# A tuned list scheduler replaced by an explicit order of all operations, and the first MLP group passed on by two token tiles

## The chip, the cores and the metric

The kernel runs on one core of one Trainium2 chip. The metric is device time in microseconds (us) of one execution, lower is better. Each kernel is run several times, and always beside runs of the kernel before on the same chip. Such runs have a state, fast or slow. A ratio is the mean time of one kernel's fast runs over that of the kernel before in the same rounds, so it isn't quite the ratio of the medians quoted beside it.

## The reference, cut to what matters

One block of a network on 2048 tokens of 640 columns: a layer norm with modulation, a long convolution by Fourier transform (length 4096) gated by `q`, a residual, then a gated MLP whose gate is mixed over tokens.

```python
h = _layernorm(x) * (1 + ca) + sa
x = x + ga * _A_ref(h, A_k, A_v, A_shift_k, A_ssm_k, A_ssm_D)   # taps, k*v, FFT convolution, times h
h = _layernorm(x) * (1 + cb) + sb
# _B_ref:
z  = _gelu(h @ w_in)
z1 = z[..., :Fh]                                 # Fh = 864
z2 = _layernorm(z[..., Fh:])                     # over Fh
g  = einsum('ts,bsf->btf', w_sp, z2) + b_sp      # "the mix": every output tile needs all 16 token tiles of z2
x  = x + gb * ((z1 * g) @ w_out)
```

## The kernel before

The first half of the kernel (convolution, second norm, MLP up to the gelu) is not written as instructions in order. It is written as about 950 operations, each with what it reads and writes, the engines that may do it, and a planned cost in ns for each engine. A list scheduler with hand-searched priorities (`WANT`, `SHIFT`, `SECOND`) then emits them one by one:

```python
while len(order) < len(ops):
    found = []
    for i in ready:
        ...                                   # earliest start on each engine that may do it
        if e == "POOL" or (e == "DVE" and o["port"]):
            at = max(at, port)                # the plan's own model of the shared port
    best = min((f for f in found if f[1] <= first + LOOK), default=None)
    ...
    if e == "PE":
        self.gap = max(0, int((at - max(last, freed[i]) - 300) * 0.7 / 217))   # dummy matmuls to keep the clock
    o["fn"](engines[e])                       # emits the instruction
```

A token group is four tiles of 128 tokens. From the second group on, the normed tokens are turned by a transposing transfer from one buffer `Z` into another:

```python
def turn(e):
    new(hT, "Z", [P, TB, ND, P])
    e.dma_start_transpose(tl[hT][...], tl[xn2][...])       # Z <- Z
op({"SP": 2900}, turn, r=[xn2], w=[hT], new=[(hT, "Z")], flip=True)
```

and each gate tile is normed on VectorE when its group's `rstdz` is there:

```python
op({"POOL": 1300}, lambda e: rstd_from_var(rstdz[...], mvz[...]), w=[("rsz", g)])   # a power, on GpSimd
for i, n in enumerate(ns):
    op({"DVE": 500}, lambda e: e.tensor_scalar(z2[i], z2[i], mvz[n], rstdz[n], op0=subtract, op1=mult), port=True)
```

What follows the plan is ordinary code, which the change leaves alone, and which the plan doesn't know:

```python
w_o = wsp_pool.tile([P, NFT, D], BF16, name="w_o")
for ft in range(NFT):                                      # 7
    nc.sync.dma_start(w_o[...], B_w_out[...])
    nc.gpsimd.tensor_tensor(w_o[...], w_o[...], gb_bf[...], op=ALU.mult)
for t in range(NT + 2):
    if t < NT: mix(t)                                      # sums over all 16 tiles of z2, tile 0 first
    ...
```

Of the kernel before, what the change touches and what calls it, by code (L numbers as in the profile page):

```python
# [9 lines left out]
ACT = mybir.ActivationFunctionType  # L10
# [29 lines left out]
LAND = 1700  # L40
LOOK = 42
# [4 lines left out]
WANT = {  # L46
    "f1": 2526.25, "m2": -2037.5, "e": -1944.5, "g2": -1880.25, "sc": -2044.75, "kv0": -1374, "kv1": 127.25,
    "kv2": 1518, "kv3": 2314.5, "kv4": -3404.75, "taps0": -2491.5, "taps1": -157, "taps2": -1900, "taps3": 1990.75,
    "taps4": 2196.25, "kvw0": -1376.75, "kvw1": 1291.5, "kvw2": -1942.25, "kvw3": 2716, "kvw4": 2479.5, "XK0": -1183,
    "XK1": -1620.25, "XK2": 2217, "XK3": 2063, "XK4": 2051.5, "XU0": -1237, "XU1": -1437.75, "XU2": 1801,  # L50
    "XU3": -1000, "XU4": -1551, "k0": -2274, "k1": 89, "k2": -860.25, "k3": -849, "k4": -2326.5, "fk0": -246,
    "fk1": -1040.5, "fk2": -2275, "fk3": -687, "fk4": -1166.75, "u0": -1617.75, "u1": -1000.75, "u2": -1876,
    "u3": -3389.75, "u4": -849.5, "x0": -165.25, "x1": -853, "x2": 1266.5, "x3": 1164, "ln": 928.25, "xn": -1205,
    "gh0": 788.5, "gh1": -1692, "gh2": 2045.75, "gh3": 1665.5, "gh4": 4149.25, "mod2": 1139.5, "mod1": 1538,
    "mod0": 2027, "silu": 3015.75, "mod3": 4190.5, "mod4": 1313, "mod5": -1137.75, "w_in1": 3051, "w_in0": -489.75,
    "zt0": 2475, "zt1": -229, "zt2": -1076.5, "zt3": -1427.5, "zt4": -1724, "y0": -2303.5, "y1": -1549, "y2": -210.5,
    "y3": -1942.5, "y4": 2310.75, "res0": -1928.75, "res1": 1888.5, "res2": 2026, "res3_0": -1974.25,
    "res3_1": -1926.75, "res3_2": 1516.5, "res3_3": -1289.25, "res4_0": 1282.75, "res4_1": 1349.25, "res4_2": 2307.5,
    "res4_3": -2318.5, "st1": 4181.5, "st3_0": 1263.25, "st3_1": 2953.5, "st3_2": 2321, "st3_3": 3037,
    "st4_0": -1125.75, "st4_1": 1295, "st4_2": -1307.25, "st4_3": -2593, "zp_0": -1343, "zp_1": -802.25,  # L60
    "zp_2": -1300.5, "zp_3": -2354.5, "zx_0": 1146, "zx_1": -299.75, "zx_2": -1879, "zx_3": -1309.25, "zf_0": -1226.5,
    "zf_1": -1880.25, "zf_2": 1818, "zf_3": -1874, "z2_0": -1075.75, "z2_1": -1726, "z2_2": -1235, "z2_3": 2149,
    "zs_0": 1156.75, "zs_1": 2527.75, "zs_2": -147.25, "zs_3": -1292.5, "zn_0": 1300.75, "zn_1": 1666.75,
    "zn_2": 1139.25, "zn_3": 1283.5, "z1_0": -1946.5, "z1_1": -1925.5, "z1_2": 1809, "z1_3": 2464.75,
}


SHIFT = {
    0: 29.25, 1: 33.25, 2: 6.25, 4: -16, 5: 31, 6: -36, 7: 19, 9: 40.25, 12: -40.75, 13: -24, 14: 34, 15: -121.5,
    16: 52.25, 17: -75.75, 18: 0.25, 20: -0.75, 21: 2.75, 22: 39.25, 23: -15.25, 24: 41.5, 25: -1, 27: 6, 28: -4.75,  # L70
    29: 96.5, 30: 8.75, 31: 10.5, 32: 17, 33: -0.5, 35: 0.75, 36: -6.75, 37: 27, 38: -5.5, 39: -1.5, 40: -30.5,
    41: -38.5, 42: -2.75, 43: -47.75, 44: -21.5, 46: 29.75, 47: 37.25, 48: -6, 49: 7.75, 50: 15.5, 51: -14.75,
    52: 11.5, 53: -104.25, 55: 4.75, 56: -9.75, 57: 6.75, 58: 11, 59: -79.25, 60: 15.5, 61: -9, 62: 52.5, 63: 131.75,
    64: 2.5, 65: 7.25, 67: -21, 68: 5, 70: -50.75, 71: 5.25, 72: -74.75, 73: -87.25, 74: 10.25, 75: -19.25, 76: -2.75,
    77: -5, 78: -11.75, 79: -0.75, 80: 1.75, 82: 9, 83: -47.75, 84: 5.75, 85: 90.75, 86: -60, 89: 159.5, 91: 0.5,
    92: -68.25, 93: -11.75, 95: -1.75, 96: 11, 97: 99.75, 98: 113, 99: -1, 100: -26.5, 101: -461.5, 102: 64.75,
    103: -36.75, 104: -24.75, 105: 53, 106: 51, 107: 183.75, 108: 70.25, 109: 10.25, 110: -104.75, 111: -11.5,
    112: 35, 114: 5.25, 116: 0.5, 117: -5.75, 120: 5.5, 121: 7.25, 122: 51.75, 123: 11, 124: -2.75, 125: -104,
    126: 63.25, 127: 44.75, 128: 110.5, 129: -35.25, 130: 97.25, 131: 64.25, 132: -82.5, 135: 3.75, 136: 0.5,
    137: 30.75, 138: -2.5, 139: 12.75, 140: 1.75, 141: 15.5, 143: -1.25, 144: -23.5, 146: 207, 147: 185.5,  # L80
    148: -16.75, 149: 29.5, 151: 39.75, 152: 23, 153: 9.5, 154: -6.5, 155: 1.75, 156: -61.5, 157: 38.75, 158: -49.25,
    159: 0.5, 160: -72.25, 161: -111.75, 162: -10, 164: -19, 165: -71, 166: -2.5, 170: 128, 171: -49.75, 172: -64.5,
    173: -77.75, 174: -4.25, 175: 0.5, 176: 51, 177: -13.5, 178: -8, 179: -27, 180: -33, 181: -207.25, 182: 5.25,
    183: -11, 185: -20.5, 186: 35.5, 187: -38.25, 189: -0.5, 192: -12.75, 193: -0.25, 194: -1.75, 196: -0.25,
    197: -13.75, 199: -12.75, 200: -21, 201: -55.25, 202: 26.75, 203: -26.75, 204: -2.75, 205: 1, 206: 21.25, 207: -1,
    208: 44.5, 209: -11.75, 210: 0.75, 211: -3.25, 214: 22.75, 216: 13, 217: -6.25, 218: -16.5, 219: 1.5, 220: 59.75,
    221: -3.25, 222: 2.5, 223: -26.25, 224: 64.5, 225: -39.25, 227: -3.75, 228: -4.25, 229: -59.75, 230: 22.25,
    231: 52.25, 232: 157.25, 235: -10, 236: 17, 237: -1.25, 238: 11.75, 239: 87.25, 240: 14.5, 241: -0.75, 242: -4.25,
    243: -8.5, 244: -9.5, 245: 3.5, 246: 1, 247: 425, 249: 35.25, 250: -5, 251: -0.5, 252: 41.5, 253: 81, 254: 1,
    256: -94.5, 257: 157.5, 259: 575.5, 260: -41.75, 263: 8.5, 265: 6.5, 266: 55, 267: -2.5, 268: 84.5, 270: -18,  # L90
    272: -5.25, 273: 101, 276: 113.5, 277: -26, 278: 15.75, 279: -26.5, 281: 10.75, 283: 32.75, 285: 6.75, 286: 63.75,
    287: 23.25, 288: 2.25, 289: -24.5, 291: -6.5, 292: 10.25, 293: 0.5, 294: -53.25, 295: 19.5, 296: 1.5, 297: 0.75,
    298: -14.75, 299: -1.5, 300: 57.25, 302: -1, 304: -42, 305: 7.25, 306: -51.25, 307: 17.75, 309: -36.75, 310: -2.5,
    311: 3, 312: 45.25, 313: 4, 314: 17.5, 315: 3.25, 317: -3.5, 318: 22, 319: 43, 320: -28.5, 321: -0.5, 322: -56.75,
    323: 345, 324: -20.25, 325: -3, 326: 103, 327: -30.25, 328: -8, 329: -0.5, 331: 24, 332: -4, 333: -23.75, 334: 8,
    335: -7.25, 338: -63.75, 340: -2, 341: -9, 342: -1.5, 343: 0.75, 344: 9.75, 345: 46, 346: 3.5, 348: -27.75,
    349: -57.25, 350: -1.5, 351: 23, 352: 9.25, 354: 3.75, 355: -0.25, 356: 155.25, 361: 37, 362: -11.75, 363: -185,
    365: 97, 366: 36, 367: -43, 368: -10.25, 370: 35.25, 371: 12.25, 373: 8, 374: 22.5, 375: -45.75, 377: 0.5,
    379: -130, 380: 1.25, 381: 0.75, 382: 6.75, 383: 15.25, 384: -3.25, 385: -13.75, 387: -4.25, 388: -6, 389: 31,
    390: -14.5, 391: -69, 392: 40, 393: 35.75, 394: -1, 395: 33, 396: 12.5, 397: 18, 398: -0.25, 399: 9.25, 400: 29,  # L100
    402: -8.25, 403: -12, 404: -9, 405: -3.5, 406: -7, 407: 0.5, 408: 3.75, 409: -21.75, 410: -7, 411: -151.25,
    412: -31.25, 414: 3.5, 415: 6.75, 416: 57, 418: 153.5, 419: -35.75, 422: -0.5, 423: -7, 424: 95.25, 425: -56.75,
    426: 10, 427: -558.5, 428: 9, 429: -20.75, 430: -49, 431: -62, 432: 4, 433: -54.25, 434: 2.5, 435: -140,
    436: -32.5, 439: 18.75, 440: -26.25, 441: 22.5, 443: 51, 445: 47.25, 447: -4.75, 448: -32.25, 449: 121.5,
    450: -10.75, 452: 44, 453: -56.25, 454: 19.5, 455: 4.25, 456: -1.75, 457: 51.75, 458: 0.75, 459: -75.25,
    461: 10.75, 462: 14, 463: -4, 464: -72.75, 465: 5.25, 466: -2.25, 468: 37.25, 469: 17.75, 472: 3, 473: -67,
    474: -5, 475: 34.25, 476: 13.25, 477: -2, 479: 47, 480: 6.25, 481: 16.25, 482: -0.25, 483: 3.25, 484: -27.75,
    485: 0.75, 486: 0.5, 488: -12.5, 489: -4.5, 490: -10.75, 491: 102.5, 492: 22.25, 495: 213, 496: -4.25, 497: -32,
    499: -28.5, 500: 8.5, 501: 165, 502: -21.5, 503: -2.5, 504: -3.75, 505: 1.25, 506: 63.75, 508: -1.5, 509: 21.5,
# [36 lines left out]
}  # L146


SECOND = {"dg": -616, "g2": -164, "gc": 12663, "gh": 4296, "h2": -6312, "ln": 876, "m1": 63, "m2": 9277, "res": 10869, "x0": 9361, "x1": 5727, "xn": 3890, "z": 2269, "zt": 17578, "zx": 970}


class Plan:



    def __init__(self):
# [952 lines left out]
```

## Time and profile before

| | us |
|---|---|
| median of the runs before the prediction | 342.29 |
| span of the profiled execution (a run of 346.58) | 344.8 |
| first transposes of the last convolution unit | 141.63 |
| first MLP matmul | 156.40 |
| first matmul of the mix | 216.19 |
| mix to end | 128.6 |

The way to read such a table is as a chain on TensorE: each line is the first moment at which TensorE can do the next part, so a gain or a loss has to appear as a shorter or longer distance between two of them. The prediction shows the lines behind it, but for the first:

```profile
141.63 0.61 PE L821 MATMUL pu<-ident,Z 128*128 128x128 bf16 x8
```

The source line of the MLP's transposing transfers (the columns of the first line are minimum, median and maximum duration in ns on the queue; the second is the time from issue to landing in us):

```profile
L949 SPq DMA_TRANSPOSE Z<-Z x3: 2481/2514/2539, 162.1 to 188.9; - x3
...
DMA to landing us min/median/max: 4.1/4.1/6.1
```

### The profile page before, as it was taken

The page shows a single profiled execution, that of the slowest core. Times are in us where ns is not written, and L with a number is a line of the kernel's source. Part 1 is how long each engine was busy: PE and PEld are TensorE (multiplying, and loading weights), DVE is VectorE, ACT ScalarE, POOL GpSimd, SP SyncE. Part 2 cuts the span into 40 slices and gives each one's busy share as a digit, 9 for nine tenths or more (in the row PEclk, how much of TensorE's full clock was granted, in tenths as well). Part 3 has the DMA queues.
Part 4 walks back from the last instruction along what each step waited for, and adds up shares of the span by engine and source line. Part 5 has one row for each costly group of instructions (what it writes and reads, how often), then busy time and mean ns, then how long its engine had stood idle before and what let it go on. Part 6 is the DMA issues. An engine that isn't in the chain of part 4 may idle for free.

```text
span 344.8 us, 6903 instructions
## 1 busy us (share of the span) xinstructions
PE 324.1 (94%) x2880; PEld 210.6 (61%) x2880; DVE 209.8 (61%) x435; ACT 139.8 (41%) x242; POOL 98.5 (29%) x112
## 2 busy tenths in 40 slices
PE   8587999999999999959999999999999999999996
PEld 3255776777878888744555555555555555555554
DVE  7797879855849898699578788622333222322323
ACT  4599678578667873713555565100000000000000
POOL 3352021599898923321120025700000000000000
PEclk9899899999999999967999999999999999999999
DMA  8799594999298938000230995067445555621211
GB/s 135 232 204 281 151 196 123 258 211 244 85 226 249 262 101 210 2 2 16 63 76 0 140 224 149 0 140 143 106 109 117 123 119 126 135 69 46 48 46 57
DMA packets 128518, 45.02 MB, mean 131 GB/s; under 512 B 117640, under 2 KB 127720, under 8 KB 128488
## 3 DMA queue, kind: packets, MB, share of 16 engines
q1 hardware_dynamic: 127832, 44.59, 57.2%
q8 instruction: 22, 0.36, 0.4%
q10 hardware_dynamic: 656, 0.01, 0.1%
q14 instruction: 8, 0.07, 0.1%
HBM read 16.11 MB, written 5.24 MB: 62 GB/s over the span
## 4 chain that ended last, share of the span: by engine, by line
PE 80%; DVE 7%; DMA 5%; ACT 4%; issue 2%; POOL 0%; DVEq 0%
PE ps L1043 27%; PE pu L385 17%; PE pz L385 17%; PE po L1061 9%; PE sm L385 7%; PE s L385 2%; DMA ZT<-Z 2%; ACT X L407 2%; DVE T L606 1%; DMA kv_scr<-big 1%; DMA X<-kv_scr 1%; DVE T L492 1%; DMA sk_bf<-in_A_shift_k_dram 1%; DVE T L490 1%; ACT KH L407 1%
## 5 line engine op out<-in xcount | busy, mean ns | idle before, releaser
L1043 PE MATMUL ps<-X,wT 128*128 128x432 bf16 x512 | 95.7, 346 | 0.0
L1043 PEld LDWEIGHTS <-wT 128*128 128x128 bf16 x512 | 50.1, 98 | 42.2
L606 DVE TENSOR_TENSOR T<-pu,KH 128x1024 bf16<-128x1024 f32 x40 | 47.6, 1218 | 8.8 <-PE pu L385 7.7
L385 PE MATMUL pu<-X,M 128*128 128x128 bf16 (+1 forms) x480 | 45.5, 240 | 4.0 <-ACT X L407 1.6
L385 PEld LDWEIGHTS <-Z 128*128 128x128 bf16 x320 | 31.8, 99 | 28.5 <-issue 1.8
L1054 ACT COPY uT<-pt 128x896 bf16<-128x896 bf16 x1 | 0.9, 907 | 118.9 <-PE pt L1053 118.9
L385 PEld LDWEIGHTS <-M 128*128 128x128 bf16 x480 | 36.4, 99 | 10.9 <-issue 5.0
L385 PE MATMUL pz<-T,G 128*128 128x128 bf16 (+1 forms) x480 | 41.3, 237 | 0.1
L1046 DVE SCALAR_TENSOR_TENSOR u<-ps,bcol,G 128x432 bf16<-128x432 f32 x18 | 12.0, 668 | 42.1 <-PE ps L1043 42.1
L385 PEld LDWEIGHTS <-G 128*128 128x128 bf16 x480 | 34.8, 98 | 3.4 <-issue 0.4
L407 ACT CAST X<-s 128x1024 bf16<-128x1024 f32 x32 | 32.7, 1023 | 6.3 <-PE s L385 6.2
L385 PE MATMUL pu<-big,Z 128*128 128x432 bf16 x160 | 33.9, 353 | 0.0
L385 PE MATMUL pz<-big,Z 128*128 128x432 bf16 x160 | 33.3, 350 | 0.0
L1061 PE MATMUL po<-w_o,uT 128*128 128x320 bf16 (+1 forms) x224 | 32.8, 299 | 0.0
L407 ACT CAST Z<-pz 128x512 bf16<-128x512 f32 x40 | 23.5, 589 | 19.2 <-PE pz L385 19.2
L1061 PEld LDWEIGHTS <-uT 128*128 128x128 bf16 (+1 forms) x224 | 21.8, 98 | 9.8
L1046 DVE SCALAR_TENSOR_TENSOR u<-ps,bcol,M 128x432 bf16<-128x432 f32 x14 | 9.3, 667 | 29.8 <-PE ps L1043 29.8
L780 POOL TENSOR_TENSOR gh<-gh,gca_bf 128x512 bf16<-128x512 bf16 x20 | 22.9, 1156 | 11.2 <-DVE gca_bf L767 11.2
L385 PE MATMUL sm<-big,dg 128*128 128x512 bf16 x80 | 22.3, 416 | 4.0 <-DVE big L674 4.0
L407 ACT CAST KH<-pu 128x512 bf16<-128x512 f32 x40 | 22.7, 598 | 5.6 <-PE pu L385 5.5
L1000 DVE BATCH_NORM_STATS2 stz<-X 128x6 f32<-128x432 bf16 x32 | 18.8, 596 | 9.5 <-ACT X L994 9.1
L1063 DVE TENSOR_TENSOR ot<-po,xt 128x320 bf16<-128x320 f32 x32 | 15.7, 492 | 13.5 <-PE po L1061 13.5
(132 smaller groups left out, 357.7 us busy)
## 6 DMA issues: line engine op xcount, KB each, us to landing
wm<-in_w_mod_dram SPq DMA_DIRECT2D x6, 800.0 KB, 5.1
xt<-in_A_q_dram SPq DMA_DIRECT2D x4, 640.0 KB, 5.4
out_dram<-ot SPq DMA_DIRECT2D x16, 160.0 KB, 2.2
big<-in_B_w_in_dram SPq DMA_DIRECT2D x2, 1080.0 KB, 6.3
X<-in_A_ssm_k_dram SPq DMA_DIRECT2D x4, 512.0 KB, 6.4
kv_scr<-big SPq DMA_DIRECT2D x4, 512.0 KB, 3.3
X<-kv_scr SPq DMA_DIRECT2D x4, 512.0 KB, 4.6
w_o<-in_B_w_out_dram SPq DMA_DIRECT2D x6, 160.0 KB, 3.3
```

Source lines behind the costliest of these rows:

```text
L385: nc.tensor.matmul(o, lhsT=w, rhs=x, start=start, stop=stop)
L407: (e.copy if e is nc.scalar else e.tensor_copy)(dst, src)
L490: e.tensor_scalar(tl[a][:, h], mbase[:], mstep[:, h * NCH + i:h * NCH + i + 1], MAGIC, op0=ALU.add, op1=ALU.add)
L492: op({"DVE": 690}, lambda e: e.scalar_tensor_tensor(tl[a][:], tl[a][:], MAGIC, mbase[:, None].to_broadcast([P, 2, KCH, QH]), op0=ALU.subtr ...
L606: e.tensor_tensor(T_[:], tl[pu][:, :, :, None, :].to_broadcast([P, KP, 2, 2, DU]), tl[KH][:, :, None, :, :].to_broadcast([P, KP, 2, 2, DU] ...
L780: lambda e, vec=vec, o=o: e.tensor_tensor(gvu, gvu, vec[:, None, d0:d0 + du].to_broadcast([P, TB, du]), op=o),
L1000: op({"DVE": 620}, lambda e, i=i, n=n, fc=fc: e.bn_stats(out=stz[:, n, fc, :], in_=tl[z2][:, i, fc * FC:(fc + 1) * FC]), r=[(z2, (i, fc))] ...
L1043: nc.tensor.matmul(ps[:, :FC], lhsT=wTs[t][:, s_, :], rhs=tl["z2_%d" % (s_ // TB)][:, s_ % TB, fc * FC:(fc + 1) * FC], start=(s_ == 0), st ...
L1046: nc.vector.scalar_tensor_tensor(u[:, sl], ps[:, :FC], bcol[:, t:t + 1], z1[t][:, sl], op0=ALU.add, op1=ALU.mult)
L1054: nc.scalar.copy(uTs[t][:], pt[:])
L1061: nc.tensor.matmul(ps[:, :HS], lhsT=uTs[t][:fsz[ft], ft, :], rhs=w_o[:fsz[ft], ft, h * HS:(h + 1) * HS], start=(ft == 0), stop=(ft == NFT ...
L1063: nc.vector.tensor_tensor(ot[:, h * HS:(h + 1) * HS], ps[:, :HS], xt[:, t, h * HS:(h + 1) * HS], op=ALU.add)
```

## The change

The search for a schedule moves out of the kernel. Its result is written down as one string, a letter for the engine and a number for the operation, and is replayed. The search could move any operation to any place, which priorities could not. The first MLP group is also passed on in two pieces of two token tiles, so that its first matmuls need only half of the last residuals and statistics.

```diff
+ORDER = """
+S9 D87 D100 D101 D5 D106 D107 D88 D94 D95 A97 D11 D6 D112 D89 S22 A96 S10 A113 D98 P12 D36 D13 A90 A109 P14 D15 A7
 ... [40 lines cut]
+A960 D967
+"""
-WANT = {...}  -SHIFT = {...}  -SECOND = {...}
 ...
+        for e, i in order:
+            o = ops[i]
+            cost, at, slot = o["eng"][e], free[e], 0.0
 ...
+        def pieces(g):
+            return [range(0, 2), range(2, 4)] if g == 0 else [range(g * TB, (g + 1) * TB)]
 ...
+    nmrz = persist.tile([P, NT], F32)
 ...
+            op({"DVE": 150}, lambda e: e.scalar_tensor_tensor(nmrz[:, gs], mvz[:, gs, 0], -1.0, rstdz[:, gs], ...))
+                    if e is nc.scalar:
+                        e.activation(z, z, ACT.Identity, bias=nmrz[:, n:n + 1], scale=rstdz[:, n:n + 1])
 ...
-LAND = 1700          +LAND = 1500
-op({"SP": 4200}, load, r=[Z], w=[ZT], ...)      +op({"SP": 3750}, load, r=[Z], w=[ZT], ...)
-op({"SP": 2900}, turn, r=[xn2], w=[hT], ...)    +op({"SP": 2600}, turn, r=[xn2], w=[hT], ...)
```

The new column tile `nmrz` (16 floats, 64 bytes in each partition) lets ScalarE take a gate norm.

## The prediction

> **What bounds the kernel now.** I read the page's busy line and its 40 slices first, then TensorE's waits, then the instructions in order of time around each hole, and last the norms at the end of the MLP.
>
> ```profile
> PE 324.1 (94%) x2880; PEld 210.6 (61%) x2880; DVE 209.8 (61%) x435; ACT 139.8 (41%) x242; POOL 98.5 (29%) x112
> ...
> PE   8587999999999999959999999999999999999996
> ...
> DVE  7797879855849898699578788622333222322323
> ACT  4599678578667873713555565100000000000000
> ...
> PEclk9899899999999999967999999999999999999999
> ```
>
> TensorE is full except in two places: the first four or five slices (to 37 us) and slice 18 (around 150 us), where the clock falls too. So the order of the first half can only win what these two places and small holes between them cost. I priced all first-half TensorE work at the warm spacing of this trace: a forward group of six matmuls every 0.44 us (80 of them: 35.4), an inverse group of twelve every 0.885 (40: 35.4), taps 0.87 (20: 17.4), the first transform 0.33 (40: 13.2), modulation, transposes and last transforms 18.6. The sum is 120.0 us. The 64 MLP groups take 0.912 each (58.4). The mix starts at 216.2, so the MLP starts, in effect, at 157.8. From the first tap at 6.57 that is 151.2 us for 120.0 of work: 31.2 us lost. By part: to 37.2 us 16.5 of work in 30.7 (lost 14.2); from there to 141.6 97.1 in 104.3 (lost 7.2); the handover from the convolution to the MLP 6.3 in 16.2 (lost 9.9).
>
> Start-up, in TensorE's waits and in 5-us windows (columns PE, PEld, DVE, ACT, POOL, clock):
>
> ```profile
> PE sm L385 <- DVE big L674: 4.0, 1, 4.0
> ...
> PE sm L962 <- DVE Z L941: 3.2, 1, 3.2
> ```
> ```profile
> 20.00:25.00 5.00, 3.86 (x40) 2.54 (x35) 4.86 (x15) 4.95 (x8) 3.29 (x6) 1.00 1.21 239
> 25.00:30.00 5.00, 4.40 (x57) 2.75 (x56) 2.92 (x12) 4.71 (x12) 1.93 (x3) 1.00 0.96 178
> 30.00:35.00 5.00, 3.41 (x36) 2.54 (x34) 4.58 (x10) 5.00 (x10) 0.00 (x0) 0.79 1.04 385
> ```
>
> First TensorE waits 4.0 for VectorE's first product with v (it is busy with sine tables), then ScalarE is the bound: 4.7 to 5.0 of every 5 us.
>
> The handover:
>
> ```profile
> 142.28 3.76 ACT L407 COPY T<-pu 128x1024 bf16<-128x1024 bf16 x4
> 145.56 0.95 PE L385 MATMUL sm<-Ebd,T 128*128 128x16 bf16 x32
> 150.47 1.03 POOL L326 TENSOR_TENSOR rstd<-rstd,mhalf 128x4 f32<-128x4 f32 x1
> 152.11 0.29 PE L962 MATMUL sm<-ident,Z 128*128 128x128 bf16 x1 [3.19 <-DVE Z L941]
> 156.40 2.00 PE L385 MATMUL pu<-big,Z 128*128 128x432 bf16 x5
> ```
>
> Four copies in series on ScalarE hold the last transform; then statistics of all four tiles, the GpSimd power, the norms, five transposes and five modulations come one after another before the first MLP matmul, which runs cold (2.00 for five).
>
> One more place costs nothing today but will matter:
>
> ```profile
> 212.00 5.88 POOL L1071 TENSOR_TENSOR w_o<-w_o,gb_bf 128x640 bf16<-128x640 bf16 x4
> 212.07 6.05 DVE L1009 TENSOR_SCALAR X<-X,mvz,rstdz 128x864 bf16<-128x864 bf16 x4 [1.18 <-POOL rstdz L326]
> 216.19 1.08 PE L1043 MATMUL ps<-X,wT 128*128 128x432 bf16 x5
> ```
>
> Four norms that take 0.45 to 0.50 elsewhere take about 1.5 each here, in step with GpSimd's scaling of the output weights. They are the tiles 13, 14, 12, 15, which the mix's sum needs last.
>
> **What the Trainium skill says.** "SBUF — State Buffer", section "SBUF: two separate sides": the port pair that VectorE and GpSimd share is an exclusive lock, held for a whole instruction. The last fence agrees: a norm is let in only between two GpSimd operations. "TensorE: Matmul & The Clock Gate", section "What's actually happening": after an idle window of about 3.4 us the array runs at half clock until it has been busy again. The trace agrees: the granted clock averages 0.54 from 150 to 160 us. "Trace Analysis", section "Optimization Strategy": where the most-contended engine changes over time, interleaving the regimes may help. That is what the new order tries where ScalarE binds. "ScalarE: Activation LUTs", section "What ACT_TABLE_LOAD costs", gives about 1283 ns for a load; the trace has 1.28 us for each of two in the ScalarE-bound stretch.
>
> **The change, part by part.** Arithmetic and the code from the mix on stay; 120.0 and 58.4 us of TensorE work stay. Dummy matmuls that keep the clock warm fall from 27 to 20, and those of the handover vanish.
>
> Start-up: VectorE's chain before the first v product loses four small table operations and gains two tap diagonals and a sign product, and it no longer starts with a wait for the tap weights; I reckon it 0.9 us earlier (10.8 instead of 11.7) if v has landed. No copy of the next k stands any more between the write of the first product and its reading, so the second first-transform can begin near 21 instead of 26.1. Six of 16 casts there go to VectorE (six times 0.52 off ScalarE), one table load (1.28 + 0.20) moves to the handover; three weight-table copies of about 1 us come the other way. But TensorE's order puts that second transform before most forward groups, so it will wait for the transfer. Net gain 3.5 (1 to 6).
>
> Middle: mixed better, no dummies; I give it 2.5 of the 7.2 lost.
>
> Handover: two of the four copies go to VectorE and a modulation product (0.70) fills the hole: about 1.6. The two-tile passage: from the start of the last transform to the MLP's effective start was 157.8 - 145.6 = 12.2. Now product 0.42, add 0.26, two statistics and two aggregates 0.95, power and scale 1.5, two norms 0.8, five half-width modulations about 2: with 1 us for the transform first, some 7.5, and the other half's transposes (0.6) come among MLP groups. 12.2 - 8.1 is 4.1. Together 5.7; I take 5.5. Against it, ten statistics of 0.41 are put off into the MLP, though 4 norms and 6 full-width modulations go to ScalarE; I take 0.5 off for a stall in the MLP. So the mix becomes ready 3.5 + 2.5 + 5.5 - 0.5 = 11.0 earlier.
>
> End of the MLP: the new VectorE order ends with seven norms after the last rstd; the sixth is tile 0, and the mix's first matmul reads tile 0: the built program has a VectorE wait on that first weight load, which before stood no earlier than the fifth. Between the last second-half group and the mix stand 13 groups (11.9 us). VectorE has then some 7 us of statistics and norms, GpSimd 1.3, so rstd ends about 2.5 to 4 before the mix could start. GpSimd then begins the seven scalings, and each norm costs 1.49 instead of 0.5: six times 1.49 is 8.9, perhaps one slot more for the small scale operation. Stall: 9.5 - 3 = 6.5 us, with 1.5 for the cold clock after an idle window: 8.0 lost. Sum: -11.0 + 8.0 = -3.0, from 342.3 to 339.3.
>
> **Rivals.** (a) The stall does not come: the output weights land later, or the norms slip in. Then 342.3 - 11.0 = 331.3. Against: in four of four cases the norm waited for GpSimd. (b) The early second transform waits so long for its transfer that start-up gains nothing, with the stall: 339.3 + 3.5 = 342.8. For it: such reads took 5.4 us to land, and a load of 640 KB now stands before it. (c) The delayed statistics make the second MLP group late, because its transpose (4.1 to landing) starts later; 1 to 3 us more, 341 or so. For it: VectorE was busy 9.1 of 10 us from 150 to 160.
>
> **Range and chances.** Gain before the mix 7 to 14, stall and clock 4 to 10, partly tied (the earlier all else, the more the norms show). That gives 333.5 to 344. Faster by over 2% needs 335.4 or less: it takes rival (a) or half of it: 0.20. Slower by over 2% (349.1) needs loss in all parts: 0.03. Within: 0.77.
>
> **What would show it.** A TensorE wait of 4 us or more at the first mix matmul, put down to VectorE's norm, with seven norms of about 1.5 us beside the scalings, and a clock dip there; the first MLP group about 4 to 6 us sooner after the last transform, without a dip; the second first-transform at 20 to 22 us, with a wait for its transfer before it; from the mix's start to the end the same 128.6 us, but for the dip. No wait at the mix makes the main step wrong; a mix ready less than 7 us sooner makes the sum of gains wrong.

## The result, and the profile after

The changed kernel takes 354.38 us (353.59 to 355.17, four runs), the kernel before in the same rounds 343.13; the ratio of the fast runs is 1.0321 (95% interval 1.0264 to 1.0378). It is slower by 3.2%. The page after:

```profile
PE 323.2 (91%) x2864; PEld 210.8 (60%) x2873; DVE 216.9 (61%) x441; ACT 146.1 (41%) x248; POOL 96.1 (27%) x112
...
PE   6668999999999989699799896799999999999996
...
PEclk9969999999999998879899999899999999999999
```

A slice is 8.8 us. Where before had one dip after the start, after has a row of them: the 15th slice (124 to 133 us), the 17th (141 to 150), the 20th (168 to 177), the 23rd (194 to 203), the 25th and 26th (212 to 230). TensorE's waits name them, in the order of their size:

```profile
PE ps L969 <- DVE X L935: 5.4, 1, 5.4
PE pz L280 <- DMA X<-kv_scr: 3.0, 1, 3.0
PE sm L853 <- DVE Z L841: 2.7, 1, 2.7
PE sm L280 <- DMA ZT<-Z: 2.3, 1, 2.3
PE pu L280 <- ACT M L912: 2.0, 1, 2.0
```

The first is the start of the mix, the second the second first-transform at 19 to 22 us, the third the handover, the fourth a transpose of the fourth unit, the fifth the first matmul of the second MLP group at 170.75 us. The label of the fifth names a gelu, but that buffer had long been free: the modulation of the second group began only when its transfer landed, and TensorE went on 0.3 us after the last of them ended:

```profile
169.06 1.38 DVE L889 TENSOR_SCALAR Z<-Z,cb_col,sb_col 128x512 bf16<-128x512 bf16 x4 [2.76 <-DMA Z<-Z]
```

The chain on TensorE, both ways, from the two profiles, with three of the lines of after:

```profile
140.31 1.06 PE L738 MATMUL pu<-ident,Z 128*128 128x128 bf16 x16
143.59 1.75 PE L280 MATMUL sm<-Ebd,T 128*128 128x16 bf16 x64
152.13 2.01 PE L280 MATMUL pz<-big,Z 128*128 128x432 bf16 x5
```

| | before | after | difference of the stretch |
|---|---|---|---|
| transposes of the last unit | 141.63 | 140.31 | -1.3 |
| first MLP matmul | 156.40 | 152.13 | -3.0 |
| last MLP matmul ends, about | 216.2 | 217.7 | +5.8 |
| first matmul of the mix | 216.19 | 223.27 | +5.6 |
| end | 344.8 | 353.4 | +1.5 |

The sum is +8.6 between these two profiles, while the medians are 11.2 apart: the profile of before is a run 3.5 us over its median, and late in the first part. In two more profiles of the same order (the controls below) the first line stands at 139.20 and 140.10, so the -1.3 is no gain. The last two stretches are the stall at the mix, which was predicted (8.0). The +5.8 inside the MLP was not. The mix's stall, in order of time (start, duration, engine; in brackets the idle time before it):

```profile
212.68 10.20 POOL L997 TENSOR_TENSOR w_o<-w_o,gb_bf 128x640 bf16<-128x640 bf16 x7
```
```profile
212.74 1.35 DVE L927 SCALAR_TENSOR_TENSOR nmrz<-mvz,rstdz 128x4 f32<-128x4 f32 x1 [1.41 <-POOL rstdz L220]
214.01 9.52 DVE L935 TENSOR_SCALAR X<-X,mvz,rstdz 128x864 bf16<-128x864 bf16 x7
```
```profile
223.27 12.99 PE L969 MATMUL ps<-X,wT 128*128 128x432 bf16 x62 [5.44 <-DVE X L935]
```

Seven norms follow the last `rstdz`. The first six take about 1.56 us each and begin 1.5 us apart, in step with the seven scalings on GpSimd; the seventh begins when the scalings have ended and takes 0.50. Tile 0 is the sixth of them; it is done at 223.12. A scale operation on four columns, 0.14 us elsewhere, takes 1.35.

### The profile page after: what moved, and what is told of

The parts are those of the page before. It is cut to its first block, busy times and chain, and to the rows that moved or that the text cites. A ratio compares the mean times of both kernels' runs of the same rounds, so it can differ in the third digit from the quotient of the medians.

```text
span 353.4 us, 6901 instructions
## 1 busy us (share of the span) xinstructions
PE 323.2 (91%) x2864; PEld 210.8 (60%) x2873; DVE 216.9 (61%) x441; ACT 146.1 (41%) x248; POOL 96.1 (27%) x112
## 4 chain that ended last, share of the span: by engine, by line
PE 73%; DVE 10%; DMA 10%; ACT 3%; issue 2%; POOL 0%; DVEq 0%; POOLq 0%; ACTq 0%
PE ps L969 27%; PE pz L280 14%; PE pu L280 13%; PE po L987 9%; PE sm L280 6%; DMA Z<-Z 4%; DVE X L935 3%; PE s L280 3%; DMA X<-kv_scr 3%; DMA ZT<-Z 2%; DMA kv_scr<-big 2%; ACT Z L887 1%; DVE T L387 1%; DVE T L501 1%; DVE T L385 1%
## 5 line engine op out<-in xcount | busy, mean ns | idle before, releaser
L969 PE MATMUL ps<-X,wT 128*128 128x432 bf16 x512 | 97.2, 349 | 5.4 <-DVE X L935 5.4
L501 DVE TENSOR_TENSOR T<-pu,KH 128x1024 bf16<-128x1024 f32 x40 | 48.1, 1222 | 11.8 <-PE pu L280 8.8
L280 PE MATMUL pz<-T,G 128*128 128x128 bf16 (+1 forms) x480 | 42.4, 241 | 0.3 <-DVE T L501 0.3
L280 PE MATMUL pu<-big,Z 128*128 128x432 bf16 x160 | 35.1, 355 | 3.1 <-ACT M L912 2.0
L280 PE MATMUL pz<-big,Z 128*128 128x432 bf16 x160 | 35.2, 359 | 0.0
L302 ACT CAST X<-s 128x1024 bf16<-128x1024 f32 x30 | 30.5, 1016 | 9.7 <-PE s L280 9.6
L302 ACT CAST Z<-pz 128x512 bf16<-128x512 f32 x36 | 21.1, 592 | 13.7 <-PE pz L280 13.7
L675 POOL TENSOR_TENSOR gh<-gh,gca_bf 128x512 bf16<-128x512 bf16 x17 | 19.7, 1174 | 14.2 <-ACT gh L622 11.0
L675 POOL TENSOR_TENSOR gh<-gh,gsa_bf 128x512 bf16<-128x512 bf16 x19 | 21.9, 1159 | 2.7 <-DVE gsa_bf L665 1.8
L918 DVE BATCH_NORM_STATS2 stz<-X 128x6 f32<-128x432 bf16 x32 | 17.9, 588 | 7.0 <-ACT X L912 7.0
```

Of the source, the lines that this page charges most:

```text
L280: nc.tensor.matmul(o, lhsT=w, rhs=x, start=start, stop=stop)
L302: (e.copy if e is nc.scalar else e.tensor_copy)(dst, src)
L501: e.tensor_tensor(T_[:], tl[pu][:, :, :, None, :].to_broadcast([P, KP, 2, 2, DU]), tl[KH][:, :, None, :, :].to_broadcast([P, KP, 2, 2, DU] ...
L675: lambda e, vec=vec, o=o: e.tensor_tensor(gvu, gvu, vec[:, None, d0:d0 + du].to_broadcast([P, TB, du]), op=o),
L918: op({"DVE": 620}, lambda e, i=i, n=n, fc=fc: e.bn_stats(out=stz[:, n, fc, :], in_=tl[z2][:, i, fc * FC:(fc + 1) * FC]), r=[(z2, (i, fc))] ...
L969: nc.tensor.matmul(ps[:, :FC], lhsT=wTs[t][:, s_, :], rhs=tl["z2_%d" % (s_ // TB)][:, s_ % TB, fc * FC:(fc + 1) * FC], start=(s_ == 0), st ...
```

## The experiments

The theory was that the search had fitted its order to a plan that is wrong in two places: it doesn't know the scalings of `w_o`, which hold the port that VectorE and GpSimd share, and its transfers are shorter than the chip's. The rivals were that the two-tile pieces cost more than they bring, and that the earlier MLP merely runs into something fixed. All kernels gave correct results.

### The mix: norms first, or the scalings elsewhere

Three kernels. The first moves four norms of older groups ahead of the last statistics by a helper that edits the string:

```diff
+def moved(names, before):
+    names = names.split()
+    left = [x for x in ORDER.split() if x not in names]
+    at = left.index(before)
+    return " ".join(left[:at] + names + left[at:])
+ORDER = moved("D769 D772 D837 D903", "D941")   # norms of groups 0 to 2, ahead of the last group's statistics
+ORDER = moved("D967", "D968")                  # tile 12 before tile 13
```

> The changed kernel with four normalisations of gate tiles put ahead of the last statistics on VectorE, so that only the last group's own three follow the last rstd power. Shared-port theory: VectorE's queue behind that power is 1.35 + 3 x 1.36 us instead of 1.35 + 7 x 1.36, tile 0 is normalised long before, so TensorE's wait at the mix (5.4 us) and the half clock after it (about 1.5 us) are gone: 347 to 348 us, against 354.4. Rival, that the MLP's end itself is late and the seven normalisations only fill the time: the wait moves to another instruction and the time stays within 1 us of 354.4.

The second leaves the order alone and gives the scalings to VectorE; the third does the same to the kernel before.

```diff
-        nc.gpsimd.tensor_tensor(w_o[...], w_o[...], gb_bf[...], op=ALU.mult)
+        nc.vector.tensor_tensor(w_o[...], w_o[...], gb_bf[...], op=ALU.mult)
```

> The changed kernel, its order untouched, with the seven scalings of w_o on VectorE instead of GpSimd. Shared-port theory: the seven normalisations take about 0.45 us each instead of 1.36, tile 0 is ready about 1.35 - 0.15 + 5 x 0.9 = 5.7 us earlier, which ends the wait at the mix: 347 to 348 us. Theory that the normalisations are slow for another reason (their number, the waits on ScalarE): they stay at 1.36 us and the time at 354, or rises by the 3 us that VectorE now spends on w_o.

> The kernel before with the same move of the w_o scalings to VectorE, as a control. In it four normalisations lie beside the scalings at about 1.5 us each and TensorE didn't wait for them, so the shared-port theory expects no gain: 342 to 344 us, within 1 us of before. If it gains 3 us or more, the scalings cost something in both kernels and the loss isn't the change's own.

Measured: norms first 346.59 us (ratio 1.0118, interval 1.0096 to 1.0140), scalings on VectorE 347.67 (1.0159, 1.0123 to 1.0196), the control 343.05 (1.0012, 0.9973 to 1.0052). The norms with the scalings on VectorE:

```profile
212.29 0.16 DVE L927 SCALAR_TENSOR_TENSOR nmrz<-mvz,rstdz 128x4 f32<-128x4 f32 x1 [1.41 <-POOL rstdz L220]
212.37 2.99 DVE L935 TENSOR_SCALAR X<-X,mvz,rstdz 128x864 bf16<-128x864 bf16 x7
```

Seven norms in 2.99 us instead of 9.52, and the small operation in 0.16 instead of 1.35: nothing but the engine of the scalings had changed. In the first kernel the norms stay slow (three in 4.64 us), but the mix no longer needs them early, and TensorE starts it with no wait. By the ratios they bring back 7.0 and 5.6 us. The intervals of the two overlap, and in both profiles the mix starts without a wait and takes 128.6 or 128.7 us to the end, so nothing is made of the difference. The control gains nothing, as expected: before, the order happened to put the norms that come late in the sum last.

### GpSimd's residual adds, alone

In the changed kernel's handover four residual adds run on GpSimd from 148 to 161 us; before, the last had ended at 147.8. They hold the same port while VectorE has hardly any idle time:

```profile
148.02 1.15 POOL L717 TENSOR_TENSOR xt<-xt,gh 128x512 bf16<-128x512 bf16 x1
...
152.36 2.26 POOL L717 TENSOR_TENSOR xt<-xt,gh 128x512 bf16<-128x512 bf16 x2
```
```profile
148.08 1.10 DVE L829 SCALAR_TENSOR_TENSOR nmr<-mv,rstd 128x2 f32<-128x2 f32 x1
...
153.45 1.35 DVE L841 TENSOR_SCALAR Z<-xt,mv,rstd 128x640 bf16<-128x640 bf16 x1
```

```diff
+ORDER = moved("G605 G604 G633 D637 D634 G547", "D677")    # behind the second group's norms
```

> The changed kernel with four residual adds of GpSimd (and two statistics that read them) put behind the normalisations of the second token group, so none lies between the transforms' end and the hand-over of the second group. In the changed kernel a VectorE add took 0.91 us beside them (0.42 for a longer one alone), nmr 1.10, 0.76 and 0.99 (0.14 alone in the kernel before), a normalisation 1.35 (0.45 alone): about 4 us on an engine without idle time there. Port theory: first MLP matmul about 1 us earlier, the second group's transposing transfer issued 2 to 4 us earlier, TensorE's 2.0 us wait for it and the slow clock behind it gone: 350 to 352 us. Rival, that the two-tile pieces or the transfers themselves bound the hand-over: under 1 us gained.

Measured: 357.55 us (1.0423, 1.0379 to 1.0467), by the ratios 1% slower than the changed kernel. The first MLP matmul did come 1.1 us earlier (151.02), with `nmr` at 0.16 us, but the rest went wrong in three ways:

```profile
158.89 0.41 DVE L872 TENSOR_SCALAR Z<-sm,cb_col,sb_col 128x256 bf16<-128x256 bf16 x1 [2.79 <-PE sm L863]
...
159.66 2.91 DVE L851 TENSOR_SCALAR Z<-xt,mv,rstd 128x640 bf16<-128x640 bf16 x3
```
```profile
170.34 4.65 PE L290 MATMUL pu<-ident 128*128 128x512 bf16 x13 [2.37 <-ACT M L922]
```

VectorE, now early, stood 2.79 us before a modulation that waits for late transposes; GpSimd, free to go on, ran the adds right beside the three norms, which took 0.97 us each; and the plan, which recomputes its gaps from the order, put 13 dummy matmuls on TensorE behind the wait. So this kernel is not a clean test of the total, and the next version had to mend all three.

### The tile that moved all others

The traces then showed something that no order explains. The MLP's transposing transfers take longer after than before, all three of them, in each of the three kernels made from the changed one so far. The view of their line after:

```profile
L881 SPq DMA_TRANSPOSE Z<-Z x3: 2992/3025/3062, 162.4 to 187.9; - x3
...
DMA to landing us min/median/max: 4.9/6.5/7.1
```

The transfer of the second group alone, in the transfer views of the 10 us from 161 to 171 (each number is a slice of 0.25 us), first before, then after:

```profile
GB/s 0 0 0 0 0 0 0 0 0 194 292 288 291 291 292 288 291 291 106 0 0 0 0 0 0 0 66 0 0 0 0 0 0 0 0 0 0 0 0 0
```
```profile
GB/s 0 0 33 0 0 0 0 0 0 0 66 224 213 210 210 215 222 215 218 222 209 218 166 79 0 0 0 0 0 0 0 0 0 0 0 0 0 0 0 0
```

Same bytes, same packets of 256 bytes, 290 GB/s against 215. What differs is the address: in the built programs the three `Z` buffers begin at a multiple of 512 bytes in each partition before, and 64 bytes past one after, because `nmrz` is allocated ahead of them. Two kernels test it, each with one line:

```diff
-    nmrz = persist.tile([P, NT], F32)
+    nmrz = persist.tile([P, 8 * NT], F32)          # changed kernel: 512 bytes instead of 64
```
```diff
     rstdz = persist.tile([P, NT], F32)
+    shift = persist.tile([P, NT], F32)             # kernel before: 64 bytes that nobody needs
+    nc.vector.memset(shift[:, 0:1], 0.0)
```

> The changed kernel with its new 64-byte column tile nmrz widened to 512 bytes, and nothing else: the order and every instruction stay, only the tiles allocated behind it move, so that the transposed tiles start at a multiple of 512 bytes again as in the kernel before (in the changed kernel at 64 bytes past one). Address theory: the three transposing transfers of the MLP run at 290 GB/s instead of 216, 2.5 us of data instead of 3.2 to 4.2, the second group's wait of 2.0 us on TensorE and the 1.1 us of half clock after it go, the wait for the last first-half transpose falls from 2.3 to about 1, the fourth group's 0.9 goes: 348 to 351 us against 354.4. Rival, that the slower transfers come from what runs beside them (the new order): the rate stays near 216 GB/s and the time at 354.

> The kernel before with an unused 64-byte column tile allocated at the place where the changed kernel has nmrz, as the opposite control. Address theory: its transposing transfers fall to about 216 GB/s and take 3.2 us of data or more. In it the second group's landing (166.2 us) had about 2 us to spare to the instruction that reads it, so the time rises by 0 to 2.5 us: 342 to 345. Rival: the rate stays at 290 GB/s and the time at 342.7.

Measured: the widened tile 349.62 us (1.0177, 1.0123 to 1.0230), against 1.0321 for the changed kernel; the shifted kernel before 344.17 (1.0028, 0.9981 to 1.0076). First the line of the transfers in the widened kernel, then in the shifted one:

```profile
L881 SPq DMA_TRANSPOSE Z<-Z x3: 2485/2499/2573, 160.7 to 183.6; - x3
...
DMA to landing us min/median/max: 4.1/4.2/5.7
```
```profile
L951 SPq DMA_TRANSPOSE Z<-Z x3: 2992/3026/3083, 160.5 to 187.0; - x3
...
DMA to landing us min/median/max: 4.9/4.9/6.1
```

The speed goes with the address both ways, with no other change but one memset of a column in the shifted kernel. It costs the kernel before nothing that is clear of noise: there the second group's transfer has slack (only TensorE's wait for the last `ZT` is longer, 1.6 us against 0.4 and 0.5). It costs the changed kernel about 1.4%, because its MLP begins 4 us earlier while the transfer is issued no earlier (162.44 against 162.08): the slack is used up. From the first MLP matmul to the end of the MLP the widened kernel takes 61.8 us, the changed one 65.5, the kernel before 59.8.

The wait of the second group was expected to go; it only fell from 2.0 to 1.2. Its transfer is the one at 5.7 in the view of the widened kernel: the data took 2.5 us, but landed 2 us after their end, as in the changed kernel (6.5), while before they landed 0.5 us after (4.1). So the address makes 0.8 of the 2.4 us by which this landing is later. In both late traces a packet of 16 KB of an instruction queue follows on the data (164.4 to 165.3 and 166.9 to 167.8) and the transfer's last packets of 4 bytes come after it; that it holds them up is not tried. In the two kernels with both repairs, below, this landing takes 4.2 and 4.1, which is what the plan has for it (2600 ns and 1500 to land): so for aligned transfers the plan's figure was right.

Three more runs ask which boundary counts, and whose address.

```diff
+    nmrz = persist.tile([P, 2 * NT], F32)          # one kernel: 128 bytes
+    nmrz = persist.tile([P, 4 * NT], F32)          # another: 256 bytes
+        nmrz = consta.tile([P, NT], F32)           # a third: 64 bytes, but allocated behind Z
```

> The changed kernel with nmrz widened to 128 bytes only, so that the transposed tiles start 128 bytes past a multiple of 512. If a multiple of 128 bytes is enough, the transposing transfers of the MLP run at 290 GB/s and the time is that of the run with 512 bytes (about 349.6 us); if it takes a multiple of 512, they stay near 216 GB/s and the time at 354.

> The changed kernel with nmrz widened to 256 bytes: the transposed tiles Z start 256 bytes past a multiple of 512. With 64 and 128 bytes past one the transfers ran at about 216 GB/s, at a multiple of 512 at 290. If 256 is the boundary that counts: 290 GB/s and about 349.6 us. If 512 is: 216 GB/s and about 354.

> The changed kernel with nmrz, at its 64 bytes, allocated behind the tiles Z, so that Z starts at a multiple of 512 as before while ZT, X, KH and the modulation weights stay 64 bytes further on. If the address of the tiles that are read (Z in both kinds of transfer) decides, the MLP's transfers and the convolution's transposes are both fast: 349.6 us, as with all of them moved. If the address of the written tile decides, the MLP's (Z into Z) are fast at 2.5 us and the convolution's (Z into ZT) stay at 5.0 us of data against 4.0: some 350 to 351.

| kernel | `Z` past a multiple of 512 | `Z` into `Z`, median ns | `Z` into `ZT`, shortest ns | us | ratio |
|---|---|---|---|---|---|
| before | 0 | 2514 | 4062 | 343.13 | 1 |
| before, shifted | 64 | 3026 | 4871 | 344.17 | 1.0028 |
| changed | 64 | 3025 | 4801 | 354.38 | 1.0321 |
| 128 bytes | 128 | 2992 | 4776 | 354.42 | 1.0337 |
| 256 bytes | 256 | 2539 | 3971 | 349.54 | 1.0145 |
| 512 bytes | 0 | 2499 | 3958 | 349.62 | 1.0177 |
| behind `Z` | 0 | 2550 | 3916 | 342.26 | 0.9932 |

A multiple of 256 bytes is enough, 128 is not. In the last kernel `ZT`, which the convolution's transfers write, still lies 64 bytes further on than before, and those transfers are fast all the same (in the built programs `ZT` doesn't start at a multiple of 256 bytes in the kernel before either). So for them it is the address of the tile that is read that counts; for the MLP's, which read and write `Z`, the runs don't part the two.

The time of the last kernel is a miss: 342.26 where 349.6 to 351 was expected, below the kernel before. The reason is in its profile at the mix:

```profile
218.08 9.52 POOL L997 TENSOR_TENSOR w_o<-w_o,gb_bf 128x640 bf16<-128x640 bf16 x7 [10.55 <-DMA w_o<-in_B_w_out_dram]
```
```profile
207.64 2.99 DVE L935 TENSOR_SCALAR X<-X,mvz,rstdz 128x864 bf16<-128x864 bf16 x7
```

The memory behind `Z` is given back after the first half, and the mix's tiles are laid into it. With `nmrz` moved there, the loads of `w_o` went out at 215.4 us instead of 204.9, so that GpSimd scaled the weights after the norms and not beside them. The built program and the trace show why: `nmrz` lies inside the fourth buffer of the mix's weights `wT`. SyncE stood before the load into that buffer from 196.2 to 211.09 us, when the last norm, on ScalarE, had ended at 211.06; the loads of `w_o` come behind it in SyncE's order. But after the two with the scalings on VectorE (in the control four norms took 1.75 us) it is a third kernel in which the norms are fast when the scalings don't lie beside them, and its stall at the mix is gone.

### Both repairs, then the adds again

The first kernel has the widened tile and the early norms. The second adds the adds, mended: three of them go into 8 us in which GpSimd had waited (134 to 142), the fourth goes to VectorE behind the second group's norms together with the late modulation, and the dummy matmuls are fixed to the changed kernel's places.

```diff
+ORDER = moved("G547 G605 G604", "G623")
+ORDER = ORDER.replace(" G633 ", " D633 ")
+ORDER = moved("D722 D633 D637 D634", "D677")
-                self.gap = max(0, int((at - max(last, slot) - 300) * 0.7 / 217))
+                self.gap = {12: 17, 131: 1, 159: 1, 173: 1}.get(i, 0)
```

> Both repairs: the widened nmrz and the four normalisations ahead of the last statistics. If the mix stall (7.8 us gained alone) and the addresses (about 4) are separate losses they add up: 341 to 344 us, level with the kernel before. If the earlier MLP only makes the last normalisations late again, 345 to 347.

> The third part added, mended: three residual adds of GpSimd put before the transforms' end, into 8 us in which GpSimd waited, the fourth given to VectorE behind the second group's normalisations, the last modulation of the first group (for which VectorE stood idle 2.8 us in the run of the adds alone) behind them too, and the dummy matmuls fixed to the changed kernel's four places so that the plan can't add any (it had put 13 in that run, 4.6 us of TensorE). Port theory of the hand-over: first MLP matmul 1 us earlier, second group's transfer issued about 3 us earlier: 1 to 2 us under the run before it, 339 to 342 us. If the hand-over isn't bound by the port: the same as the run before it.

Measured: 342.02 us (0.9970, 0.9924 to 1.0016) and 339.89 us (0.9888, 0.9849 to 0.9927). The two losses add up: 1.0321 less 1.0118 and 1.0321 less 1.0177 make 0.0347, and the run with both repairs took off 0.0351. With the adds out of the way the handover is shorter still, though the intervals of the two versions just touch, and the second bundles four edits. VectorE in the last kernel:

```profile
144.73 0.16 DVE L843 SCALAR_TENSOR_TENSOR nmr<-mv,rstd 128x2 f32<-128x2 f32 x1
...
154.34 0.16 DVE L843 SCALAR_TENSOR_TENSOR nmr<-mv,rstd 128x4 f32<-128x4 f32 x1 [1.13 <-POOL rstd L234]
154.42 1.16 DVE L855 TENSOR_SCALAR Z<-xt,mv,rstd 128x640 bf16<-128x640 bf16 x3
```

From the last unit's transposes to the first MLP matmul: 14.8 us before, 11.8 in the changed kernel, 10.9 here; the MLP 59.8, 65.5, 60.3. This version beats both kernels, the one before by 1.1%.

### One half of the order at a time

Two hybrids, both with the widened tile: the new order up to the last unit's transposes and then the old one with whole groups, and the other way round (with the early norms).

```diff
 ORDER = """          # 610 operations that stand before that point in both kernels, in the order of one;
 ...                  # all others in the order of the other
```

> A hybrid with aligned tiles: the new order up to the transposes of the last convolution unit, from there the order of the kernel before, with the first MLP group in one piece. In the profiles with aligned tiles the new order reached that point 2 to 3 us earlier than the kernel before. If that gain is the first part's own and the rest keeps it: 341 to 342.5 us, 1.5 to 2.5 under the kernel before of the same rounds. If the state the new first part leaves behind (statistics and adds put off) costs the old rest as much: level with before.

> The other hybrid, aligned and with the four normalisations early: the old order up to the same point, from there the new one with the first group in two pieces. The pieces' theory: hand-over 2.9 us shorter, of which the MLP gives back 1.9: 0.5 to 1.5 us under before. Rival, that the pieces cost more than they bring (more and smaller instructions on VectorE): 1 us or more over before.

Measured: 345.16 us (1.0052, 1.0017 to 1.0087) and 343.78 (1.0007, 0.9975 to 1.0039). The first was a miss: its handover took 16.4 us, 1.6 more than before, about what its first part had gained (137.96 against 139.20 and 140.10 in the controls). The second is level, at the edge of what was expected. So neither half shows a gain alone. Nor do the pieces show a cost: the interval leaves room for 1.3 us at most, while the chain itself is shorter with them (handover 11.9 us against 14.8, MLP 61.5 against 59.8). How the 1.1% of the best version divides between the halves stays open at this size.

### A load of x behind the second transform's

```diff
+ORDER = moved("S462", "A141")     # on top of the best version
```

> The best version so far (aligned, four normalisations early, adds moved) with one load of x put behind the first half of the second transform's load, which shared the DMA engines with it. TensorE waited 2.2 us for that transfer at 20 us. If the sharing is what makes it late: that wait falls by about 1 us and the time to 338 to 339.5 us; if it is the round trip through DRAM itself: the same as before the edit, 340 us.

Measured: 340.56 us (0.9916, 0.9865 to 0.9967), not apart from the version without it. The wait for that transfer went from 2.2 us to two of 0.9 and less, and two waits of TensorE for VectorE, of 1.5 and 1.0 us, appeared around it. The start stays bound by more than one thing.

## Why the prediction was wrong

The prediction was 339.3, the range ended at 344.0, and a loss of over 2% had a chance of 0.03. By its own steps:

**The mix's stall, -8.0: right.** Seven norms in step with the scalings, tile 0 the sixth, a wait of 5.4 us (6.5 predicted), a clock dip, and 1.5 us more from the mix to the end. Two of its terms were off and partly made up for each other: from the end of the last `rstdz` to tile 0 it took 10.4 us, not 9.5, and TensorE still had 5.0 us of work there, not 3. Three kernels removed it in three ways.

**Start-up, +3.5: wrong; rival (b) came true.** The second first-transform did come at 21 to 22 us, but behind a wait of 3.0 us for its transfer. I had also measured the start from one profile that was late there. Count the time lost as in the prediction, as time less warm TensorE work, but from the start of the span: when some 20 us of that work were done, the profile of before had lost 20.8, two further runs of the same order (the controls) 19.1 and 18.8, and the changed kernel 19.3 (worked out from the traces with the prediction's spacings; good to some tenths). Start-up gained nothing.

**Middle, +2.5: about half at its best, then lost.** At 105 us of TensorE's work the changed kernel had lost 23.3, the two controls 24.5 or more. Then came the wait of 2.3 us for the last transposed unit, whose transfer took 5.46 us on the queue; with `Z` aligned 3.96, and the wait 1.8.

**Handover, +5.5: right in mechanism, mis-sized; it measured 3.0.** The copies brought 0.65 of 1.6 (from the transposes to the last transform 3.93 us before, 3.28 after), the two-tile passage 2.3 of 4.1 (from there to the first MLP matmul 10.84 and 8.54). In the passage I added the durations of VectorE's operations alone, and left out that four adds moved by the new order hold the port beside them: taking them away gave 0.9 us more. The clock dip that should have vanished also stayed (0.77 from 150 to 160 us, 0.54 before). The rest is not parted.

**MLP, -0.5: this is the step that failed; it measured -5.8.** I put it down to delayed statistics, as rival (c) did for 1 to 3 us. The second group's transfer was indeed issued late for an MLP that starts 4 us sooner. But I took its 4.1 us to landing from the kernel before; after, it took 6.5, of which the address, moved by one 64-byte tile, explains 0.8, and the fourth group waited as well. With aligned tiles the MLP costs 2 us more than before instead of 5.8, so 3.7 is the address. With both repairs it takes 61.6 us, and with the adds mended too 60.3, which is 0.5 over before: the size that was predicted, but no run tests that it is the delayed statistics.

So the sum of gains before the mix was 1.3 (only because the profile of before was late) + 3.0 - 5.8 instead of 11.0, that is, -1.5. Some 5 us of the difference are the address, shown by one line. The rest is start-up, the middle and the port.

I cited the port's lock, and applied it to the end of the MLP only. I did not apply to the handover what I knew, and did not look at where the buffers lie. For that, the Trainium skill had the page: "DMA: Bandwidth & Descriptors", section "How a descriptor splits into AXI transactions", says that a read transaction must start at an address aligned to 256 bytes, and that a descriptor that doesn't start there fetches bytes that it doesn't use. A packet of 256 bytes then needs a second transaction (worked out from its rule). The runs agree as to the boundary: 0 and 256 fast, 64 and 128 slow, with packets of 256 bytes. That this is the mechanism is an inference from the boundary.

## What to carry to other kernels

An order found by search can use up the slack of the plan that it was searched on, so what the plan leaves out (work that follows it on another engine, a transfer's real time to landing) can become a stall, as both did here; replay such an order only after its plan has been compared with a trace of that very order. When a small tile is added ahead of large ones, compare the start addresses of everything that transfers read, and the duration of each kind of transfer, before blaming the schedule. Where VectorE is full, look at what GpSimd does beside it: an operation of 0.14 us took 1.35.

## What the Trainium skill lacked or had wrong

- "DMA: Bandwidth & Descriptors", section "How a descriptor splits into AXI transactions", gives no cost in time and doesn't mention transposing transfers, and no figure of the page for these is given by address. The runs show 2.5 us against 3.0 for 0.66 MB and 4.0 against 4.8 for the convolution's. Counted by the page's rule, a packet of 256 bytes should take 8 beats when aligned, 10 at 64 bytes past the boundary and 12 at 128 (worked out, not stated there); the runs show 64 and 128 alike (3025 and 2992 ns).
- The same page, section "DMA Transpose (X-bar)", lists 32-byte alignment as the requirement. It is enough for correctness, but the rate was 290 GB/s with the tiles `Z` at a multiple of 256 bytes and about 215 at 64 bytes past one.
- "Perfetto Trace Analysis" has nothing on comparing tile addresses between two versions of a kernel. Here the whole of a 4.8 us loss was in them, and no instruction differed.
